# Causal masks for four pairs of heads in one GpSimd selection, and half of a zero-padded operand made by GpSimd where ScalarE made it

## The chip, the cores and the metric

The kernel runs on one core of a Trainium2 chip. The metric is the time of one execution on the device in microseconds. The engines are TensorE (PE in the profile; its weight loads are PEld), VectorE (DVE), ScalarE (ACT), GpSimd (POOL) and the DMA queues, most of which are issued by SyncE (SP).

## What is computed

Two mixers read the same `x` of 2048 rows and 512 columns, and a gate adds them row by row:

```python
g = sigmoid((x * gate_w).sum(-1, keepdims=True))
# A: Fourier mixing, real part
a = x @ dft_hid_re.T;  b = x @ dft_hid_im.T
A = dft_seq_re @ a - dft_seq_im @ b
# B: attention with 32 heads of 16 columns, each row looks at itself and the 255 rows before it
q, k, v = heads(x @ wqkv)
s = q @ k.T * 16 ** -0.5
s = where(0 <= row - col < 256, s, -1e9)
B = merge(softmax(s) @ v) @ wo
out = g * A + (1 - g) * B
```

All data are float32. Most products are made as three products of a high and a low part (`hi`, `lo`).

## The kernel before

**Two streams on one TensorE.** The attention loop in the body of the kernel runs over `n` and is the frame. The dense work (projections, Fourier products) is a Python generator, `dense()`; between two attention matmuls the loop calls `fill(n)`, which takes the next few dense matmuls from it. TensorE's order is that of the program text (`manual_schedule`); the order on the other engines is set by the scheduler, so that a change in one place can move instructions elsewhere. Each engine works its queue in order.

**The attention.** There are 4 groups of 8 heads (4 pairs `p`), and in each group 32 blocks of 64 rows: 128 blocks, numbered `n` and, 20 blocks later, `k = n - LAG`. A block is taken twice.

- *S pass*, `s_pair(n, p)`: 64 query rows of two heads against up to 320 keys, one matmul (line 325). VectorE adds the mask and takes the row minimum (line 327), ScalarE takes the exponential and sums it (line 330). Only the row maximum and the sum are kept. `ml_rows` (lines 335 to 344) writes them out, and `m_ring` puts the maxima as extra rows beneath `ring[0]`.
- *T pass*, `t_pair(k, p)`: 64 keys of two heads against up to 320 queries, one matmul (line 388), with the maxima taken off through the extra rows. ScalarE writes the exponential to `pt` (line 389), which has four buffers. After each odd pair, GpSimd sets the two triangles outside the window to zero with `affine_select`: for each half of the partitions one selection at the front of the strip (line 394) and, if the strip is 320 wide, one at its end (line 398). One selection covers 64 partitions, two pairs and 64 columns: 128 elements a partition.
- *PV*, `pv(j)`: after the third pair of every third block `k` (`k % 3 == 0`) the matmuls of the blocks `k-3`, `k-2`, `k-1` with V (line 415), which read the masked `pt`. V comes from DRAM by two DMAs for four blocks (`v_load`), and GpSimd spreads it into `vpad` (`v_spread`, line 378).

**The pads.** The two heads of a pair lie in the same partitions, 16 rows each in turn. `make_pad(i, n)` makes the weights of a block: four pairs of 64 columns for head 0 and 64 for head 1, with the other head's rows set to zero by a factor of 0 or 1 per partition (`half`). `i = 0` is for the S pass, `i = 1` for the T pass. Both halves of the S pad and the first half of the T pad are made by VectorE (line 310), the second half of the T pad by ScalarE (line 308). There are two buffers of each; the pad of block `k+1` is called for after the first pair of block `k`, and can be written when the last T matmul of block `k-1` has read its buffer.

**PSUM.** The S and T matmuls and a few others share four banks (`ps_a`); the dense products have two (`ps_d`), PV has two (`ps_o`). A matmul waits until VectorE or ScalarE has read what was in its bank.

**Dense evictions** that come up below: `split_psum` (lines 84, 86 and 88) writes a product as a high part (ScalarE) and a low part (VectorE); `split` (lines 80 and 81) does the same for weights that were loaded.

Of the kernel before, what the change touches and what calls it, by code (L numbers as in the profile page):

```python
# [9 lines left out]
AF = mybir.ActivationFunctionType  # L10
OP = mybir.AluOpType
# [7 lines left out]
NG = 4  # L19
NP = 4  # L20
BQ = 64
NB = S // BQ
# [10 lines left out]
def fnet_window_mix(ctx: ExitStack, tc: tile.TileContext, xT, x, wqk, wv, wr, wi, cr, ci, wo, gw, out):  # L33
    nc = tc.nc
# [23 lines left out]
    def f(ap):  # L58
        return ap.bitcast(F32)
# [7 lines left out]
    @contextmanager  # L67
    def behind(*engines):
        with ExitStack() as es:
            for e in engines:  # L70
                if e in last:
                    es.enter_context(tc.issue_after(last[e]))
            yield
# [51 lines left out]
    with tc.manual_schedule(engines={mybir.EngineType.Activation, mybir.EngineType.DVE, mybir.EngineType.SP}):  # L125
# [12 lines left out]
        for dk in range(DK):  # L138
            c = slice(dk * 256, dk * 256 + 256)
# [22 lines left out]
    half = const.tile([P, 2], F32, name="half")  # L162
    mrow = const.tile([P, 2], F32, name="mrow")
    for t, edges in ((half, ((0, 16, 32, 48, 64, 80), (16, 32, 48, 64, 80, 96))), (mrow, ((96, 98), (98, 100)))):
        nc.gpsimd.memset(t, 0.0)
        for h in range(2):
            for i, e in enumerate(edges[h]):
                a = t[:, h:h + 1]
# [130 lines left out]
    def make_pad(i, n):  # L299
        if not 0 <= n < NG * NB:  # L300
            return
        t = pads[i][n % NPAD]
        b = n % NB
        with behind(*(("act", "dve") if n < NPAD else ())):
            for h in range(2):
                src, dst = f(ring[i][:96, :, b * BQ:(b + 1) * BQ]), t[:96, :, 64 * h:64 * h + 64]
                if i and h:
                    nc.scalar.activation(dst, src, AF.Copy, scale=half[:96, h:h + 1])  # L308
                else:
                    nc.vector.tensor_scalar(dst, src, half[:96, h:h + 1], None, op0=OP.mult)  # L310
        PAD[i, n] = t
# [69 lines left out]
    def t_pair(n, p):  # L381
        q0 = n % NB * BQ
        w = min(WIN, S - q0)
        if p == 0:
            PT[n] = at.tile([P, NP, WIN], F32, name="pt", bufs=4)
        pt = PT[n]
        ps = ps_a.tile([P, 512], F32, name="t", tag="st")
        nc.tensor.matmul(ps[:, :w], PAD[1, n][:, p], ring[0][:, p, q0:q0 + w], start=True, stop=True)  # L388
        nc.scalar.activation(pt[:, p, :w], ps[:, :w], AF.Exp, scale=-1.0)  # L389
        if p % 2:  # L390
            ph = slice(p - 1, p + 1)
            for h in (0, 64):
                a = pt[h:h + 64, ph, 0:64]
                nc.gpsimd.affine_select(a, a, pattern=[[0, 2], [1, 64]], compare_op=OP.is_ge, fill=0.0,  # L394
                                        base=0, channel_multiplier=-1)
                if w == WIN:
                    a = pt[h:h + 64, ph, 256:320]
                    nc.gpsimd.affine_select(a, a, pattern=[[0, 2], [-1, 64]], compare_op=OP.is_gt, fill=0.0,  # L398
                                            base=0, channel_multiplier=1)

    def pv(n):
# [310 lines left out]
    for n in range(N + LAG + 2):  # L712
# [14 lines left out]
        if n == 0:  # L727
            make_pad(0, 0)
        for p in range(NP):
            if n < N:  # L730
                s_pair(n, p)
            fill(n)
            if 0 <= k < N:
                t_pair(k, p)
            if p == 0:
                make_pad(0, n + 1)
                if k >= -1:
                    make_pad(1, k + 1)
            fill(n)
            if p == 2 and sent < maxima and n >= taken[sent] + 2:  # L740
                m_ring(sent)
                sent += 1
            if p == 2 and k % 3 == 0:
                for j in range(k - 3, k):
                    if 0 <= j < N:
                        pv(j)
                if maxima < 16 and n > 8 * maxima + 8:
                    ml_rows(maxima)
                    maxima += 1
                    taken.append(n)  # L750
# [47 lines left out]
```

## Time and profile before

| | us |
|---|---|
| median of 3 runs | 871.07 |
| lowest and highest of them | 869.48, 871.13 |
| the profiled execution | 873.39 |
| its span, first to last instruction | 871.3 |

The profile is of the profiled execution, which took 873.39 us, of which 871.3 lie between the first and the last instruction. In a group's row stand the line, the engine, the operation, the tiles and shapes, the count, then the busy time and the mean duration in ns, then the idle time of the engine ahead of these instructions with what ended most of it. In a timeline's row stand the start and the duration in us, and in brackets the idle time ahead of it with what ended it. In a chain's row stand the start and the length in us of a piece of the chain that ended last. In a row of stages stand the stretch, its length, and for PE, PEld, DVE, ACT and POOL the busy time with the number of instructions, then the granted clock of TensorE, the busy share of the DMA engines and GB/s.

The T pass begins at 106.5 us and ends at 752, the S pass ends at 660; what is left is dense work and the output projection.

### The profile page before, as it was taken

The numbers are of one execution on the slowest core, as the hardware profiler recorded it, in microseconds if no ns is written. First come the engines' busy times: TensorE is split into PE (matmuls) and PEld (weight loads), VectorE is DVE, ScalarE is ACT, GpSimd is POOL, SyncE is SP. The second block draws the span as 40 slices with busy tenths as digits, with TensorE's granted clock in tenths as the row PEclk, the third lists the DMA queues.
The fourth block names the chain that finished last, engine by engine and source line by source line (L and its number), as shares of the span: only waits on it lengthen the run. The fifth ranks groups of instructions, "written<-read, shape, count | busy, mean of one in ns | idle before, by whom it ended". The sixth has DMA issues, their size and how long they took to land.

```text
span 871.3 us, 17146 instructions
## 1 busy us (share of the span) xinstructions
PE 860.5 (99%) x5160; PEld 690.3 (79%) x5160; DVE 611.3 (70%) x1974; ACT 580.9 (67%) x1793; POOL 384.6 (44%) x1067
## 2 busy tenths in 40 slices
PE   8999999999999999999999999999999999999998
PEld 6888778787877778878788887878778787788886
DVE  4588987667878987878787777788876444564431
ACT  4388799888897987878788777877776454111110
POOL 9100054545444756656456566554546665200000
PEclk9999999999999999999999999999999999999999
DMA  6875796464749436644445354599944333485541
GB/s 229 266 226 155 248 262 197 153 214 158 241 158 289 130 105 225 172 130 135 134 131 170 105 163 133 156 349 256 329 148 159 123 118 114 130 263 192 189 145 48
DMA packets 93132, 157.87 MB, mean 181 GB/s; under 512 B 27120, under 2 KB 36080, under 8 KB 93040
## 3 DMA queue, kind: packets, MB, share of 16 engines
q1 hardware_dynamic: 92288, 155.61, 56.5%
q10 hardware_dynamic: 752, 1.18, 0.4%
q8 instruction: 40, 0.66, 0.3%
q14 instruction: 52, 0.43, 0.2%
HBM read 106.69 MB, written 50.07 MB: 180 GB/s over the span
## 4 chain that ended last, share of the span: by engine, by line
PE 92%; DVE 3%; DMA 2%; ACT 1%; issue 1%; SPq 0%; DVEq 0%; ACTq 0%
PE dc L446 40%; PE dab L266 9%; PE s L325 8%; PE o L415 8%; PE dqk L244 8%; PE t L388 8%; PE t L669 5%; PE dv L266 4%; DVE sm L327 1%; PE s L232 1%; DMA raw<-x 1%; ACT sm L330 1%; DMA ring<-qk_scr 1%; PE s L337 1%; DMA pt<-xT 0%
## 5 line engine op out<-in xcount | busy, mean ns | idle before, releaser
L446 PE MATMUL dc<-big,hi 128*128 128x512 f32 x1024 | 355.4, 395 | 0.0
L394 POOL TENSOR_SCALAR_AFFINE_SELECT pt<-pt 64x128 f32<-64x128 f32 x512 | 191.9, 375 | 276.4 <-ACT pt L389 261.2
L330 ACT ACTIVATE sm<-sm,ml 128x320 f32<-128x320 f32 (+4 forms) x512 | 277.3, 543 | 49.4 <-DVE ml L327 48.0
L327 DVE CUSTOM_DVE_ANT_0 sm<-s,mask 128x320 f32<-128x320 f32 (+4 forms) x512 | 230.7, 462 | 82.7 <-PE s L325 62.5
L389 ACT ACTIVATE pt<-t 128x320 f32<-128x320 f32 (+4 forms) x512 | 208.7, 412 | 89.8 <-PE t L388 86.2
L446 PEld LDWEIGHTS dc<-big,hi 128*128 128x128 f32 x1024 | 186.3, 188 | 32.6 <-issue 2.4
L446 PE MATMUL dc<-big,lo 128*128 128x512 f32 x512 | 201.6, 394 | 0.0
L398 POOL TENSOR_SCALAR_AFFINE_SELECT pt<-pt 64x128 f32<-64x128 f32 x448 | 161.9, 361 | 0.1
L325 PE MATMUL s<-ring,pad 128*128 128x320 f32 (+4 forms) x512 | 159.0, 310 | 0.9 <-DVE ml L327 0.5
L388 PE MATMUL t<-ring,pad 128*128 128x320 f32 (+4 forms) x512 | 155.1, 303 | 1.6 <-DVE ml L327 0.9
L310 DVE TENSOR_SCALAR pad<-ring,half 96x256 fp32r<-96x256 f32 x384 | 121.6, 358 | 24.2 <-PE t L388 22.0
L325 PEld LDWEIGHTS s<-ring,pad 128*128 128x128 f32 x512 | 96.0, 188 | 36.6 <-issue 7.4
L388 PEld LDWEIGHTS t<-ring,pad 128*128 128x128 f32 x512 | 96.1, 188 | 21.6 <-DVE ml L327 2.6
L446 PEld LDWEIGHTS dc<-big,lo 128*128 128x128 f32 x512 | 96.3, 188 | 10.6
L81 DVE TENSOR_TENSOR lo<-raw,hi 128x512 fp32r<-128x512 f32 x146 | 99.6, 712 | 1.4 <-PE dc L446 1.3
L330 ACT ACTIVATION_READ_ACCUMULATOR sm<-sm,ml 128x1 f32 x512 | 98.8, 193 | 0.0
L266 PE MATMUL dab<-hi,big 128*128 128x512 f32 x256 | 90.9, 396 | 0.0
L244 PE MATMUL dqk<-big,hi 128*128 128x512 f32 x240 | 86.7, 394 | 0.6 <-DVE hl L86 0.5
L80 DVE CAST hi<-raw 128x512 fp32r<-128x512 f32 x142 | 58.6, 453 | 38.3 <-PE dc L446 37.1
L415 PE MATMUL o<-pt,vpad 128*32 128x320 f32 (+4 forms) x1408 | 73.8, 351 | 0.0
L378 POOL COPY vpad<-vr 64x256 f32<-64x256 f32 x64 | 26.0, 405 | 91.1 <-DMA vr<-v_scr 72.0
L308 ACT ACTIVATE pad<-ring,half 96x256 fp32r<-96x256 f32 x128 | 64.1, 500 | 0.0
(82 smaller groups left out, 780.3 us busy)
## 6 DMA issues: line engine op xcount, KB each, us to landing
qk_scr<-hl SPq DMA_DIRECT2D x32, 512.0 KB
ring<-qk_scr SPq DMA_DIRECT2D x32, 512.0 KB
raw<-cr SPq DMA_DIRECT2D x32, 512.0 KB
raw<-ci SPq DMA_DIRECT2D x32, 512.0 KB
ab_scr<-hl SPq DMA_DIRECT2D x20, 512.0 KB
big<-ab_scr SPq DMA_DIRECT2D x20, 512.0 KB
r_scr<-ev SPq DMA_DIRECT2D x36, 256.0 KB
ev<-r_scr SPq DMA_DIRECT2D x36, 256.0 KB
```

The costliest lines, as they stand in the source:

```text
L244: nc.tensor.matmul(ps, w[a][:, c:c + 128], XT[dk, ss][:, b], start=n == 0, stop=n == 11)
L266: nc.tensor.matmul(ps, XT[dk, ss][:, a, c * 128:(c + 1) * 128], wh[b], start=n == 0, stop=n == 11)
L310: nc.vector.tensor_scalar(dst, src, half[:96, h:h + 1], None, op0=OP.mult)
L325: nc.tensor.matmul(ps[:, :w], PAD[0, n][:, p], ring[1][:, p, k0:k0 + w], start=True, stop=True)
L327: mark("dve", nc.vector.tensor_tensor_reduce(out=sm[:, :w], in0=ps[:, :w], in1=mask[:, WIN - w:], scale=1.0, scalar=3e38, op0=OP.add, op1= ...
L330: mark("act", nc.scalar.activation(sm[:, :w], sm[:, :w], AF.Exp, bias=nm[:, c], scale=-1.0, accum_out=l[:, c]))
L388: nc.tensor.matmul(ps[:, :w], PAD[1, n][:, p], ring[0][:, p, q0:q0 + w], start=True, stop=True)
L389: nc.scalar.activation(pt[:, p, :w], ps[:, :w], AF.Exp, scale=-1.0)
L394: nc.gpsimd.affine_select(a, a, pattern=[[0, 2], [1, 64]], compare_op=OP.is_ge, fill=0.0, base=0, channel_multiplier=-1)
L398: nc.gpsimd.affine_select(a, a, pattern=[[0, 2], [-1, 64]], compare_op=OP.is_gt, fill=0.0, base=0, channel_multiplier=1)
L415: nc.tensor.matmul(OT[g, sb][32 * p:32 * p + 32, q - sb * 512:e - sb * 512], v2[:, p], pt[:, p, q - q0:e - q0], start=first, stop=kb == 8 ...
L446: nc.tensor.matmul(ps, w[a][:, i % 8 * 128:i % 8 * 128 + 128], ab[SC[i]][:, b], start=i == ends[0] and a + b == 0, stop=i == ends[1] and a ...
```

## The change

The second half of the T pad is made by GpSimd with `tensor_scalar`, as VectorE makes the first, where ScalarE made it with a scaled copy. And in two of three blocks (`n % 3 != 2`, the last block left out) the masks are set once for all four pairs, after the last pair, so that a selection covers 256 elements a partition, and there are half as many; in the other blocks, whose PV comes soonest, the masks are set after each odd pair as before.

```diff
             for h in range(2):
                 src, dst = f(ring[i][:96, :, b * BQ:(b + 1) * BQ]), t[:96, :, 64 * h:64 * h + 64]
                 if i and h:
-                    nc.scalar.activation(dst, src, AF.Copy, scale=half[:96, h:h + 1])
+                    nc.gpsimd.tensor_scalar(dst, src, half[:96, h:h + 1], None, op0=OP.mult)
                 else:
                     nc.vector.tensor_scalar(dst, src, half[:96, h:h + 1], None, op0=OP.mult)
@@
         nc.scalar.activation(pt[:, p, :w], ps[:, :w], AF.Exp, scale=-1.0)
-        if p % 2:
-            ph = slice(p - 1, p + 1)
+        joint = n % 3 != 2 and n < NG * NB - 1
+        if p == 3 or p == 1 and not joint:
+            c = 4 if joint else 2
+            ph = slice(p + 1 - c, p + 1)
             for h in (0, 64):
                 a = pt[h:h + 64, ph, 0:64]
-                nc.gpsimd.affine_select(a, a, pattern=[[0, 2], [1, 64]], compare_op=OP.is_ge, fill=0.0,
+                nc.gpsimd.affine_select(a, a, pattern=[[0, c], [1, 64]], compare_op=OP.is_ge, fill=0.0,
                                         base=0, channel_multiplier=-1)
                 if w == WIN:
                     a = pt[h:h + 64, ph, 256:320]
-                    nc.gpsimd.affine_select(a, a, pattern=[[0, 2], [-1, 64]], compare_op=OP.is_gt, fill=0.0,
+                    nc.gpsimd.affine_select(a, a, pattern=[[0, c], [-1, 64]], compare_op=OP.is_gt, fill=0.0,
                                             base=0, channel_multiplier=1)
```

In the changed program the lines behind line 389 have moved by two: the selections stand in lines 396 and 400, PV in line 417, and the output projection in line 671. TensorE, as the comparison of the two programs' orders shows, gets the same matmuls in the same order.

## The prediction

> **What bounds the kernel now.** I read the page first: busy shares, then the shares of the chain of work that ended last, then the groups of the instructions that the change touches.
>
> ```profile
> span 871.3 us, 17146 instructions
> ...
> PE 860.5 (99%) x5160; PEld 690.3 (79%) x5160; DVE 611.3 (70%) x1974; ACT 580.9 (67%) x1793; POOL 384.6 (44%) x1067
> ...
> PE 92%; DVE 3%; DMA 2%; ACT 1%; issue 1%; SPq 0%; DVEq 0%; ACTq 0%
> ...
> L394 POOL TENSOR_SCALAR_AFFINE_SELECT pt<-pt 64x128 f32<-64x128 f32 x512 | 191.9, 375 | 276.4 <-ACT pt L389 261.2
> ...
> L310 DVE TENSOR_SCALAR pad<-ring,half 96x256 fp32r<-96x256 f32 x384 | 121.6, 358 | 24.2 <-PE t L388 22.0
> ...
> L398 POOL TENSOR_SCALAR_AFFINE_SELECT pt<-pt 64x128 f32<-64x128 f32 x448 | 161.9, 361 | 0.1
> ...
> L378 POOL COPY vpad<-vr 64x256 f32<-64x256 f32 x64 | 26.0, 405 | 91.1 <-DMA vr<-v_scr 72.0
> L308 ACT ACTIVATE pad<-ring,half 96x256 fp32r<-96x256 f32 x128 | 64.1, 500 | 0.0
> ```
>
> PE carries 92% of the chain. GpSimd and ScalarE are 44% and 67% busy, so taking work from them shortens nothing by itself: only what PE loses while it waits can be won. PE's instruction order is the same in both programs (the comparison of their orders shows no moved row). So the second view is PE's busy time by stage, and the third the chain's long pure stretch, for PE's undisturbed rate.
>
> ```profile
> 105.00:128.00 23.00, 22.30 (x120) 17.02 (x121) 20.77 (x70) 21.34 (x69) 11.47 (x33) 1.00 0.93 266
> 128.00:660.00 532.00, 529.65 (x3463) 423.64 (x3462) 421.34 (x1468) 439.52 (x1408) 290.71 (x830) 1.00 0.59 183
> ```
> ```profile
> 758.84 21.12 PE dc L446 x92
> ```
>
> In the two stages with attention PE is idle for 0.70 and 2.35 us, at full clock (1.00). A matmul of 512 columns follows the last one after 21.12 / 92 = 0.23 us while its own record is 0.40 long, so a visible idle time hides 0.17 more, and the matmul behind it takes 0.41 instead of 0.31. With some eight such waits, all that could be won is about 3.05 + 8 x 0.27 = 5.2 us. The waits of the T matmuls (line 388), where the moved pad is read, and of the PV matmuls (line 415), where the masks are needed (columns: us, times):
>
> ```profile
>   DVE ml L327: 3.5, 9
>   ACT pt L389: 1.5, 4
>   ACT pad L308: 1.4, 2
> ```
> ```profile
>   POOL pt L398: 1.6, 5
> ```
>
> These are idle times of the weight load, which runs ahead of the matmuls; PE itself loses part of them. GpSimd is almost never what PE waits for, and VectorE, which the change leaves its work, is waited for most.
>
> **The change part by part.** *ScalarE* loses 128 pads of 0.50 us: 64.1 us, from 580.9 to 517. That counts only where a pad stands in front of something PE waits for. I found four places.
>
> (a) The first T matmul, at 106.5:
>
> ```profile
> 106.06 0.41 ACT pad L308
> ```
> ```profile
> 106.52 0.41 PE L388 MATMUL t<-ring,pad 128*128 128x320 f32 x1 [0.52 <-ACT pad L308]
> ```
> ```profile
> 109.66 1.45 DVE L81 TENSOR_TENSOR lo<-raw,hi 128x512 fp32r<-128x512 f32 x2
> 111.67 0.39 PE L388 MATMUL t<-ring,pad 128*128 128x320 f32 x1 [0.18 <-DVE ml L327]
> ```
>
> The loss is 0.52 + 0.17 + 0.10 = 0.8 us. On GpSimd the first two pads wait only for loads and are ready early, so it goes. But what is late next is VectorE, which has a backlog here (20.77 of 23 us busy) and holds PE at 111.67 whether PE comes early or not. I count the 0.8 as given back there: 0.
>
> (b) At 213 PE waits for line 86, which stands behind line 81 on VectorE:
>
> ```profile
> 212.50 0.68 DVE L81 TENSOR_TENSOR lo<-raw,hi 128x512 fp32r<-128x512 f32 x1
> 213.10 0.68 DVE L86 TENSOR_TENSOR hl<-dqk,hl 128x512 fp32r<-128x512 f32 x1
> ```
> ```profile
> 213.84 0.73 PE L244 MATMUL dqk<-big,hi 128*128 128x512 f32 x2 [0.53 <-DVE hl L86]
> ```
>
> In the changed program's order line 86 stands ahead of line 81 and of one pad at this place, so it comes at least 0.6 us sooner: the 0.53 + 0.16 + 0.10 = 0.8 us go.
>
> (c) At 302 and (d) at 576 a pad stands in the row of ScalarE's instructions that ends in PE's wait:
>
> ```profile
> 300.91 0.50 ACT L308 ACTIVATE pad<-ring,half 96x256 fp32r<-96x256 f32 x1
> ```
> ```profile
> 302.33 0.41 PE L325 MATMUL s<-ring,pad 128*128 128x320 f32 x1 [0.31 <-ACT pt L389]
> ```
> ```profile
> 576.05 0.40 ACT pad L308
> ...
> 579.25 0.41 PE s L325
> ```
> ```profile
> 578.80 0.40 PE L446 MATMUL dc<-big,lo 128*128 128x512 f32 x1
> ```
>
> (c) loses 0.31 + 0.17 + 0.10 = 0.58; the pad holds the chain for 0.40, so 0.5 go with the restart. (d) loses 579.25 - 578.80 - 0.23 = 0.22 and 0.10; 0.3 go. For waits too small to show on PE (4 times 1.5 us of the weight load on line 389) I take another 0.3, between 0 and 0.8. ScalarE's part: -0.8 - 0.5 - 0.3 - 0.3 = -1.9 us.
>
> *The masks.* Of 128 blocks 85 become joint: 75 with four selections and 10, at the ends of the groups, with two, 320 of 256 elements; the other 43 keep 37 x 8 + 6 x 4 = 320 of 128. Before there were 960. A selection's price by size:
>
> ```profile
> L153 POOL TENSOR_SCALAR_AFFINE_SELECT mask<-mask 64x320 f32<-64x320 f32 x2 | 0.9, 450 | 0.1
> ```
> ```profile
> 119.69 0.39 POOL L378 COPY vpad<-vr 64x256 f32<-64x256 f32 x1 [4.30 <-DMA vr<-v_scr]
> 120.39 0.45 POOL L378 COPY vpad<-vr 64x256 f32<-64x256 f32 x1 [0.31 <-DMA vr<-v_scr]
> 120.91 0.29 POOL L394 TENSOR_SCALAR_AFFINE_SELECT pt<-pt 64x128 f32<-64x128 f32 x1
> ...
> 124.13 0.30 POOL L398 TENSOR_SCALAR_AFFINE_SELECT pt<-pt 64x128 f32<-64x128 f32 x1
> ```
> ```profile
> 120.53 0.31 PE L388 MATMUL t<-ring,pad 128*128 128x320 f32 x1
> 123.58 1.82 PE L415 MATMUL o<-pt,vpad 128*32 128x320 f32 x24
> ```
>
> 0.29 at 128 and 0.45 at 320 elements give 0.40 at 256. With the means' stretch of 375 / 290 = 1.29 all masks come to 320 x 0.40 x 1.29 + 320 x 0.37 = 283 us, 71 below the 354 of lines 394 and 398.
>
> *The pad on GpSimd* has no row. Nearest is the copy of 256 elements, 0.40 alone (405 mean); upper end 1.3, a short mask's time beside a busy VectorE; lower end 0.3, the same mask alone:
>
> ```profile
> 610.45 1.30 POOL L394 TENSOR_SCALAR_AFFINE_SELECT pt<-pt 64x128 f32<-64x128 f32 x1
> ```
>
> I take 0.42: 54 us, GpSimd 385 - 71 + 54 = 368. The Trainium skill ("GPSIMD Engine Reference", section "Engine selection") advises against elementwise work there: about half VectorE's speed with two inputs, roughly line rate with one. By its worse figure the pad would take 2 x 0.358 = 0.72 (an estimate), and the sum would be 0.6 worse; no run here shows it yet.
>
> What hides it in the steady stage: a pad may start when the T matmuls two blocks back are done, and GpSimd then idles for the exponentials (261 us in all). Around the PV group at 246:
>
> ```profile
> 244.01 0.29 POOL L394 TENSOR_SCALAR_AFFINE_SELECT pt<-pt 64x128 f32<-64x128 f32 x1 [1.57 <-ACT pt L389]
> ...
> 244.84 0.30 POOL L398 TENSOR_SCALAR_AFFINE_SELECT pt<-pt 64x128 f32<-64x128 f32 x1
> 246.31 1.23 PEld L415 LDWEIGHTS o<-pt,vpad 128*32 128x32 f32 x24 [0.36 <-issue]
> ```
>
> The pad falls into the 1.57 us. Behind it in GpSimd's queue stand the masks of the block whose last T matmul it waits for, and these wait for that matmul's exponential, which comes later still. The masks end at 245.14, 1.2 us ahead of the group and 2.3 ahead of its third block, the only one that reads them. The third block of each group keeps its masks in two parts, and the joint ones are read a block later. Cost: 0. The wait for GpSimd that T matmuls now carry is a wait for something long done; 0.
>
> At the start it isn't hidden. GpSimd's queue stands until the V loads land (119.69, 120.39). Before, half of block 1's masks were done ahead of that; in the changed order all of block 1's stand behind both copies and one pad, and a second pad stands ahead of block 2's last masks. From 120.39: pads and copies to 120.95, four joint masks 1.6, four short 1.2, a pad 0.4, four short 1.2: 125.4, to 125.9 with VectorE's stretch, instead of 124.43. The third PV block starts at 123.58 + 1.82 x 2/3, less the tail of the last record, about 124.7. PE is held by 0.7 to 1.2: +0.9. The pad between the two copies ends at 120.5, just when PE wants it at 120.53: inside that sum.
>
> **Sum:** -1.9 + 0.9 = -1.0. The profiled execution took 873.39 us for its span of 871.3; it would take 872.4. The median of the unprofiled runs is 871.07, 2.3 below; there I forecast **870.1**, with a range of its own from 868.9 to 871.3 (the start between +0.5 and +1.5, ScalarE's part between -2.7 and -1.2).
>
> **The rivals.**
>
> *1. The relief is larger.* (a) is kept because VectorE also runs ahead, the V loads land sooner as PE does, and a part of the DVE waits (3.5 us) goes since ScalarE frees buffers sooner. For it: 64 us off an engine that is 440 of 532 us busy. Against: VectorE's own load stays. Price: -0.8 for (a), no start cost, -1.9, -0.9 of the DVE waits: -3.6, **867.5**.
>
> *2. GpSimd becomes late: slower.* Its pads stand in order ahead of masks. If one takes 1.3 us, two more at the start cost 1.8; and the five PV groups that already wait for a mask are held about 0.3 longer each, 1.5 together. +0.9 + 1.8 + 1.5 - 1.9 = +2.3, **873.4**. It decides from about 1.1 us a pad. For it: masks average 375 against 290 alone. Against: the copy, as large, averages 405. The skill's same page (section "Specifications") says GpSimd shares its SBUF interface with VectorE, with contention when VectorE runs a 2-port mode or two SBUF inputs; the stretched masks agree with it.
>
> *3. It does not do what it says.* PE's order is unchanged, and each freed wait turns into one for VectorE within a block, as at (a), while the start's loss and the gain at (b) cancel: **871.1**.
>
> **How the numbers follow.** A difference under 0.2% (1.7 us) is about what a measurement of this kernel cannot tell from none. Forecast 0.53, of which 0.11 lies below 869.3; rival 1 0.24; rival 2 0.13; rival 3 0.10. Faster 0.11 + 0.24 = 0.35; same 0.42 + 0.10 = 0.52; slower 0.13. The range 867.4 to 872.9 leaves out half of rival 1 and most of rival 2, some 0.2.
>
> **What would show it.** After the change: no ACT row of line 308, 128 GpSimd rows of it with a mean near 0.42; GpSimd's masks near 283 us; the PE waits at 106, 213 and 302 gone; a new wait of line 417's matmuls for GpSimd near 125 of about 0.9; PE still waiting near 111 for VectorE. The forecast is wrong if the pad's mean is above 1 us, if T matmuls wait for GpSimd in the steady stage, or if the PE waits of VectorE shrink as well.

## The result, and the profile after

The changed kernel is slower: 876.01 us (median of 6 runs, 874.0 to 876.69) against 870.11 us (868.44 to 871.13) for the kernel before on the same chip, a ratio of 1.0065 with a 95% interval of 1.0049 to 1.0081. The forecast was 870.1. The profiled execution of the changed kernel took 876.69 us for a span of 875.0.

The page of the changed kernel, the lines that answer to those of before:

```profile
span 875.0 us, 16814 instructions
...
PE 863.1 (99%) x5160; PEld 689.3 (79%) x5160; DVE 631.0 (72%) x1974; ACT 541.0 (62%) x1665; POOL 451.5 (52%) x875
...
PE 91%; DVE 3%; DMA 2%; issue 2%; POOL 1%; ACT 0%; SPq 0%; DVEq 0%; POOLq 0%
...
L308 POOL TENSOR_SCALAR pad<-ring,half 96x256 fp32r<-96x256 f32 x128 | 142.0, 1109 | 151.2 <-PE t L388 136.6
...
L396 POOL TENSOR_SCALAR_AFFINE_SELECT pt<-pt 64x256 f32<-64x256 f32 (+1 forms) x342 | 145.6, 426 | 34.7 <-ACT pt L389 22.6
...
L310 DVE TENSOR_SCALAR pad<-ring,half 96x256 fp32r<-96x256 f32 x384 | 143.6, 414 | 22.1 <-PE t L388 20.7
...
L400 POOL TENSOR_SCALAR_AFFINE_SELECT pt<-pt 64x256 f32<-64x256 f32 (+1 forms) x298 | 131.0, 439 | 0.0
```

Read the mean of line 308 first: a pad on GpSimd takes 1.109 us, not 0.42. GpSimd's work has grown from 384.6 to 451.5 us where the forecast had it fall to 368. The masks came out as forecast: 145.6 + 131.0 = 276.6 us (283 foreseen). And VectorE's own pads, which nobody touched, went from 358 to 414 ns, 384 times: 22.0 us more on the engine that PE waits for most.

Where did PE lose the time? The stages of the two kernels, before and then after (stretch, length, busy time of PE, PEld, DVE, ACT and POOL with counts, granted clock, DMA share, GB/s):

```profile
0.00:15.00 15.00, 11.27 (x32) 8.26 (x33) 9.00 (x14) 7.00 (x13) 13.88 (x23) 0.89 0.61 199
102.00:128.00 26.00, 25.25 (x134) 19.22 (x133) 23.77 (x79) 23.27 (x76) 11.47 (x33) 1.00 0.90 264
...
268.00:660.00 392.00, 390.18 (x2537) 311.58 (x2536) 317.96 (x1102) 318.26 (x1018) 225.12 (x608) 1.00 0.59 180
```
```profile
0.00:15.00 15.00, 13.03 (x47) 9.63 (x48) 8.65 (x16) 8.07 (x15) 13.75 (x25) 1.00 0.66 222
102.00:128.00 26.00, 23.51 (x116) 16.97 (x116) 19.93 (x68) 18.90 (x60) 11.09 (x22) 0.93 0.84 248
...
268.00:660.00 392.00, 388.66 (x2521) 308.33 (x2520) 330.10 (x1091) 291.45 (x932) 263.89 (x489) 1.00 0.59 178
```

The first row is a trap. In before's profiled execution the clock was at 0.89 in the first 15 us and PE did 32 matmuls there, not 47; that execution is some 3.3 us late ahead of anything that the change touches. So positions are compared from the first T matmul on. It stands at 106.52 less its wait of 0.52 in before, so at 106.00, and at 102.63 after. What counts then is the second row, the start of the T pass: 116 matmuls in 26 us, not 134. It shows the place and not the size, since the T pass begins 3.4 us later in before's window; the size is counted from the first T matmul on.

GpSimd's timeline of the changed kernel there (start, duration, what ended the idle time ahead of it), and then PE's:

```profile
117.50 0.48 POOL L378 COPY vpad<-vr 64x256 f32<-64x256 f32 x1 [7.51 <-DMA vr<-v_scr]
117.97 0.91 POOL L308 TENSOR_SCALAR pad<-ring,half 96x256 fp32r<-96x256 f32 x1
118.94 0.40 POOL L378 COPY vpad<-vr 64x256 f32<-64x256 f32 x1
119.41 0.41 POOL L396 TENSOR_SCALAR_AFFINE_SELECT pt<-pt 64x256 f32<-64x256 f32 x1
...
122.31 0.92 POOL L308 TENSOR_SCALAR pad<-ring,half 96x256 fp32r<-96x256 f32 x1
123.19 0.46 POOL L396 TENSOR_SCALAR_AFFINE_SELECT pt<-pt 64x128 f32<-64x128 f32 x1
...
124.73 0.74 POOL L400 TENSOR_SCALAR_AFFINE_SELECT pt<-pt 64x128 f32<-64x128 f32 x1
```
```profile
102.63 0.39 PE L388 MATMUL t<-ring,pad 128*128 128x320 f32 x1
...
118.94 0.42 PE L388 MATMUL t<-ring,pad 128*128 128x320 f32 x1 [1.78 <-POOL pad L308]
...
123.16 2.14 PE L417 MATMUL o<-pt,vpad 128*32 128x320 f32 x20
125.53 0.73 PE L417 MATMUL o<-pt,vpad 128*32 128x320 f32 x4 [0.23 <-POOL pt L400]
126.91 0.31 PE L388 MATMUL t<-ring,pad 128*128 128x320 f32 x1
```

GpSimd stands idle for 7.51 us with a V copy at the head of its queue, until the load lands at 117.50. Behind that copy stands the pad of block 3 (0.91), for which PE waits 1.78 us. Then come the second copy, the masks of block 1, half those of block 2, the pad of block 4 (0.92), and the last masks of block 2, which end at 125.47. The third PV block needs these. PE comes to the T matmul behind that PV group at 126.91 - 102.63 = 24.28 us after the first T matmul. In before it came there at 126.05 - 106.00 = 20.05:

```profile
126.05 0.31 PE L388 MATMUL t<-ring,pad 128*128 128x320 f32 x1
```

The start has lost 4.2 us, where the medians of all runs differ by 5.9. From here to the last T matmul, which begins at 751.95 in before and at 755.65 after, the profiled execution loses 2.8 us more (628.74 for 625.90).

### The profile page after: what moved, and what is told of

Read it like the earlier page. It is cut to its first block, busy times and chain, and to the rows that moved or that the text cites. A ratio compares the mean times of both kernels' runs of the same rounds, so it can differ in the third digit from the quotient of the medians.

```text
span 875.0 us, 16814 instructions
## 1 busy us (share of the span) xinstructions
PE 863.1 (99%) x5160; PEld 689.3 (79%) x5160; DVE 631.0 (72%) x1974; ACT 541.0 (62%) x1665; POOL 451.5 (52%) x875
## 4 chain that ended last, share of the span: by engine, by line
PE 91%; DVE 3%; DMA 2%; issue 2%; POOL 1%; ACT 0%; SPq 0%; DVEq 0%; POOLq 0%
PE dc L448 39%; PE dqk L244 9%; PE dab L266 9%; PE s L325 9%; PE o L417 8%; PE t L388 8%; PE dv L266 5%; PE t L671 5%; DVE sm L327 1%; DVE pad L310 1%; DMA big<-ab_scr 1%; PE s L337 1%; DMA ab_scr<-hl 1%; DVE lo L81 1%; PE s L232 0%
## 5 line engine op out<-in xcount | busy, mean ns | idle before, releaser
L308 POOL TENSOR_SCALAR pad<-ring,half 96x256 fp32r<-96x256 f32 x128 | 142.0, 1109 | 151.2 <-PE t L388 136.6
L396 POOL TENSOR_SCALAR_AFFINE_SELECT pt<-pt 64x256 f32<-64x256 f32 (+1 forms) x342 | 145.6, 426 | 34.7 <-ACT pt L389 22.6
L310 DVE TENSOR_SCALAR pad<-ring,half 96x256 fp32r<-96x256 f32 x384 | 143.6, 414 | 22.1 <-PE t L388 20.7
L400 POOL TENSOR_SCALAR_AFFINE_SELECT pt<-pt 64x256 f32<-64x256 f32 (+1 forms) x298 | 131.0, 439 | 0.0
```

Of the source, the lines that this page charges most:

```text
L308: nc.gpsimd.tensor_scalar(dst, src, half[:96, h:h + 1], None, op0=OP.mult)
L396: nc.gpsimd.affine_select(a, a, pattern=[[0, c], [1, 64]], compare_op=OP.is_ge, fill=0.0, base=0, channel_multiplier=-1)
```

## The experiments

My theory after the result: GpSimd's pad is dear, and it costs time at this one place, where two pads stand in GpSimd's queue among masks and behind a load. Rivals: the joint masks come too late for PV; the price is paid all along, through VectorE's stretched pads. Ratios are to the kernel before in runs on the same chip, with 95% intervals; in brackets the medians.

**1. The pads alone on GpSimd, the masks as before.** Only the first hunk of the diff.

> Only the pad moves to GpSimd; the masks stay in selections of two pairs. Theory A (the pad is what costs: 1.0 us each on GpSimd, one of them behind the V loads at the start, and VectorE's own pads stretched): +4 to +7 us against the kernel before, line 308 near 1.1 us, line 310 near 0.41 us, a T matmul waiting for line 308 near 117 us. Theory B (the joint masks come too late): within 1 us of before. Theory C (only the start costs): +3 to +4 us.

Measured: 1.0043, 1.0027 to 1.0059 (874.29 us). PE's waits for GpSimd (total, times, longest):

```profile
PE o L415 <- POOL pt L398: 1.4, 1, 1.4
...
PE t L388 <- POOL pad L308: 0.9, 1, 0.9
```

Two waits, both at the start, where the clock was full (1.00):

```profile
102.00:128.00 26.00, 23.11 (x120) 16.95 (x120) 20.99 (x72) 19.90 (x62) 14.73 (x35) 1.00 0.89 256
```

PE comes to the T matmul behind the PV group 126.28 - 103.18 = 23.10 us after the first one, against 20.05 in before: 3.05 of the 4.2 us. The pads alone do most of the harm. By time, 0.43% or 3.7 us, the run lies in theory C's range and just under theory A's.

**2. The joint masks alone, the pads on ScalarE.** Only the second hunk.

> Only the joint masks; ScalarE keeps the pad. Theory A: within 1 us of before, GpSimd near 320 us busy, PE held at the start by at most 0.5 us. Theory B: +4 to +7 us, with PV matmuls waiting for line 400. Theory C: within 1 us.

Measured: 1.0012, 1.0000 to 1.0024 (872.25 us), with no wait of PE for GpSimd. That the joint masks come too late for PV isn't what costs 5.9 us: they cost 1.0 us (0 to 2.1).

**3. The first five T pads on ScalarE again.**

```diff
-                if i and h:
+                if i and h and n < 5:
+                    nc.scalar.activation(dst, src, AF.Copy, scale=half[:96, h:h + 1])
+                elif i and h:
                     nc.gpsimd.tensor_scalar(dst, src, half[:96, h:h + 1], None, op0=OP.mult)
```

> The changed kernel, but ScalarE makes the T pads of blocks 0 to 4, so that no pad stands in GpSimd's queue around the V loads at the start. Theory A: the wait of 1.8 us near 117 goes and 3 to 4 us come back; +2 to +3 us against before stay, as VectorE's pads stay stretched (line 310 near 0.41 us) and PE waits for VectorE at 458, 536, 577, 614 and 642 us stay. Theory C: all of it comes back, -1 to +0.5 us against before. Theory B: +5 us stay.

Measured: 1.0014, 1.0004 to 1.0023 (872.13 us). Five of 128 pads carry 1.0065 - 1.0014 = 0.51%, 4.4 us. The other 123 take as long as ever (1109 ns in the mean). What stays against before, 1.2 us (0.3 to 2.0), is less than theory A's 2 to 3 and more than theory C's 0.5.

**4. GpSimd copies its pad half instead of multiplying** (this leaves out the zeroing of the other head's rows).

```diff
-                    nc.gpsimd.tensor_scalar(dst, src, half[:96, h:h + 1], None, op0=OP.mult)
+                    nc.gpsimd.tensor_copy(dst, src)
```

> The changed kernel, but GpSimd copies the second half of the T pad and does not multiply it by the factor of 0 or 1, so that the other head's rows are left in. It measures what the multiplication costs on GpSimd. Theory A: line 308 falls from 1.1 us to 0.42 us, line 310 goes back to near 0.36 us; the wait at the start shrinks by 0.6 us and the later waits for VectorE mostly go: +1 to +3 us against before. If the size and not the operation sets the price, line 308 stays at 1 us and the time at +6 us.

Measured: 1.0009, 0.9996 to 1.0021 (871.12 us). The groups of the pad and of VectorE's pads:

```profile
L310 DVE TENSOR_SCALAR pad<-ring,half 96x256 fp32r<-96x256 f32 x384 | 134.4, 390 | 22.9 <-PE t L388 21.2 <-DMA ring<-qk_scr 1.2
L308 POOL CAST pad<-ring 96x256 fp32r<-96x256 f32 x128 | 64.9, 507 | 170.6 <-PE t L388 159.1 <-DMA ring<-qk_scr 7.2 <-issue 1.6
```

At half the price and in the same place, most of the loss is gone. The two pads that count at the start take 0.39 and 0.65 us, near the 0.42 that I had put into the sum, and even so the run is 0.8 us slower than before (-0.3 to +1.8) where the sum had -1.0, and a little under theory A's 1 to 3. VectorE's pads go back only half the way (390 ns, 358 before). In its profiled execution (872.55 us) PE still waits for GpSimd at the start, 0.37 us for a pad and 1.38 for the masks, and the T matmul behind the PV group comes 125.50 - 103.05 = 22.45 us after the first one: 2.4 us lost there, where the sum had 0.9.

**5. GpSimd multiplies by the constant 1.0** instead of by the column of factors (leaves out the same zeroing).

```diff
-                    nc.gpsimd.tensor_scalar(dst, src, half[:96, h:h + 1], None, op0=OP.mult)
+                    nc.gpsimd.tensor_scalar(dst, src, 1.0, None, op0=OP.mult)
```

> The changed kernel, but GpSimd multiplies its half of the T pads by the constant 1.0 instead of by the factors of the rows, read from a column of memory (it leaves out the zeroing of the other head's rows). If it is the read column that makes the pad 0.91 us where a copy of the same tile takes 0.51 us in the run with copies: the pad falls to about 0.5 us and the time to 871 to 872 us. If it is the multiplication itself: the pad stays near 1.1 us in the mean and the time at 875 to 877 us.

Measured: 1.0042, 1.0027 to 1.0058 (874.22 us).

```profile
L308 POOL TENSOR_SCALAR pad<-ring 96x256 fp32r<-96x256 f32 x128 | 121.2, 947 | 156.9 <-PE t L388 144.6 <-DMA ring<-qk_scr 7.0 <-issue 1.6
```

947 ns, against 1109 with the column and 507 for the copy: most of the price is the multiplication itself on this engine, the read column is the smaller part. The mean lies between the two that were expected, and the time just under the 875 to 877 us of the second.

**6. Only the two pads on ScalarE that stand in the way**, those of blocks 3 and 4 (`if i and h and n in (3, 4):` in the diff of experiment 3).

> The changed kernel, but ScalarE makes its half of two T pads again, those of blocks 3 and 4; GpSimd keeps the other 126. My theory (two pads at the start cost nearly all: the one behind the V copies, for which the T matmul of block 3 waits 1.8 us, and the next one, which stands ahead of the masks of block 2): 871.7 to 872.8 us, as with the first five pads on ScalarE, and no wait of a T matmul for GpSimd over 0.2 us. Rival (the price is paid all along, a little in every block): 875 to 876.5 us.

Measured: 1.0019, 1.0010 to 1.0029 (871.91 us), and PE waits for GpSimd nowhere. Two pads of 128 account for 0.46%, 4.0 us.

**7. All pads on GpSimd, but nothing queued behind the load.** The copies of the second V load are put behind the first pads and masks (`mark` notes an instruction, `behind` makes the next ones follow it).

```diff
-                    nc.gpsimd.tensor_scalar(dst, src, half[:96, h:h + 1], None, op0=OP.mult)
+                    mark("pool", nc.gpsimd.tensor_scalar(dst, src, half[:96, h:h + 1], None, op0=OP.mult))
...
-            nc.gpsimd.tensor_copy(v2[r, :, :, 16 * h:16 * h + 16], raw[r].rearrange("r j (p d) -> r j p d", d=16))
+            with behind(*(("pool",) if n == 4 else ())):
+                nc.gpsimd.tensor_copy(v2[r, :, :, 16 * h:16 * h + 16], raw[r].rearrange("r j (p d) -> r j p d", d=16))
```

The two selections are marked in the same way.

> The changed kernel with all pads on GpSimd, but the copies of the second V load are put behind the pads and masks of the first blocks in GpSimd's order, so that nothing of these waits for the load. If the start's loss comes from the order (a pad and the masks queued behind a load that lands at 117.5): no T matmul waits for GpSimd, the masks of block 2 end some 3 us earlier, and the time is 871.5 to 872.8 us. If it comes from the sum of GpSimd's work at the start, whatever its order: 874 to 876 us.

Measured: 1.0012, 1.0001 to 1.0024 (871.58 us). GpSimd's timeline, and then the T matmuls around the PV group:

```profile
112.00 0.92 POOL L308 TENSOR_SCALAR pad<-ring,half 96x256 fp32r<-96x256 f32 x1 [1.97 <-PE t L389]
...
116.94 0.92 POOL L308 TENSOR_SCALAR pad<-ring,half 96x256 fp32r<-96x256 f32 x1 [0.54 <-PE t L389]
...
118.86 0.29 POOL L401 TENSOR_SCALAR_AFFINE_SELECT pt<-pt 64x128 f32<-64x128 f32 x1
119.22 0.85 POOL L379 COPY vpad<-vr 64x256 f32<-64x256 f32 x2
```
```profile
102.67 0.39 PE L389 MATMUL t<-ring,pad 128*128 128x320 f32 x1
...
120.34 1.82 PE L418 MATMUL o<-pt,vpad 128*32 128x320 f32 x24
122.81 0.31 PE L389 MATMUL t<-ring,pad 128*128 128x320 f32 x1
```

The same two pads at the same 0.92 us are now made 6.0 and 5.4 us earlier, in time that GpSimd had spent standing behind a V copy whose load had not landed; block 2's masks end at 119.15 and not at 125.47. PE comes to the T matmul behind the PV group 122.81 - 102.67 = 20.14 us after the first one, against 20.05 in before. So the start's loss goes with the order alone, as it goes in experiment 6 with the two pads alone: it takes both, the pad's price and its place behind the load.

**8. The pads again apart from VectorE's**, to see whether the stretch of VectorE's pads is the rest of the loss. On the basis of experiment 3, GpSimd's half is called for two pairs of heads later from block 5 on.

```diff
-                    make_pad(1, k + 1)
+                    make_pad(1, k + 1, (0, 1) if k < 4 else (0,))
+            if p == 2 and k >= 4:
+                make_pad(1, k + 1, (1,))
```

> The changed kernel with the first five T pads on ScalarE (872.13 us), and from block 5 on GpSimd's half is issued two pairs of heads later than VectorE's half, so that they no longer run side by side. Theory of the shared memory path (VectorE's pads are stretched from 0.36 to 0.41 us by GpSimd's, and that is the rest of the loss, about 1.2 us): VectorE's pads fall to 0.36 to 0.38 us in the mean and the time to 870.7 to 871.5 us. Rival (the rest of the loss has another cause, or the stretch only passes to VectorE's other work): 871.8 to 873 us, with the pads shorter all the same.

Measured: 1.0021, 1.0010 to 1.0032 (872.27 us), VectorE's pads 414 ns. It tells nothing of the question: the scheduler places the pad by when its buffer is free, and the order on every engine is that of experiment 3. As a repeat of that kernel it gives 1.0021 for 1.0014, which shows how far the steady part can be read. One thing differs: PE waits 0.79 us for a mask in its first PV group, with no pad of GpSimd ahead of it, and in experiment 3's profile it does not. There the V copies began 13.18 us after the first T matmul, here 13.76.

**9 to 11. What is left, taken apart.** The order edit of experiment 7 on the pads alone, on the masks alone, and on the kernel before.

> The pads alone on GpSimd, masks as before, with the copies of the second V load put behind the pads and masks of the first blocks. With the copies in their old place the pads alone cost 0.43%. If the order at the start is what makes the pads dear: a ratio of 0.9990 to 1.0020 (869.1 to 871.8 us). If the eight short masks of block 2, 2.4 us instead of the joint ones' 1.7 us in each block, hold the start as well: 1.003 or more. The rest of the loss of the repaired kernel (0.12%) belongs to the pads if this run shows about 1.0010 and the masks alone show 1.0000.

> The joint masks alone, ScalarE's pads as before, with the copies of the second V load behind the masks of the first blocks. If the joint masks cost nothing but their place at the start: 0.9990 to 1.0006. If the rest of the repaired kernel's loss (0.12%) is the masks': about 1.0012.

> The kernel before, with the copies of the second V load behind the masks of the first blocks and nothing else. Nothing waits for GpSimd at the start of the kernel before, so the order alone should be worth nothing: 0.9992 to 1.0008. If the order itself gains or costs time, this run shows how much of the repaired kernels' times is the order's.

Measured: the pads alone 1.0003, 0.9994 to 1.0012 (870.23 us); the masks alone 1.0006, 0.9998 to 1.0015 (870.14 us); the kernel before 1.0000, 0.9991 to 1.0008 (869.79 us). The order by itself is worth nothing, and with it each edit costs nothing that can be told from zero. With their old order the pads alone had cost 0.43%.

**12. Each GpSimd pad from block 5 on written twice**, on the basis of experiment 7 (`for _ in range(2 if n >= 5 else 1):` ahead of the marked pad).

> The repaired kernel (all pads on GpSimd, second V copies behind the first masks; ratio 1.0012), with each of GpSimd's pads from block 5 on written twice. If GpSimd's pads cost time in the steady part through VectorE, whose own pads run beside them: VectorE's pads go above 0.43 us in the mean and the time to 873 us or more (1.003). If the steady part has room for 1.1 us more a block on GpSimd and the loss lies elsewhere: 871 to 872 us (1.001 to 1.002).

Measured: 1.0150, 1.0136 to 1.0163 (882.8 us); by the ratios 1.38%, some 12 us, more than experiment 7.

```profile
PE t L390 <- POOL pad L309: 3.8, 10, 0.6
PE t L390 <- DVE ml L328: 2.6, 6, 1.5
```
```profile
L311 DVE TENSOR_SCALAR pad<-ring,half 96x256 fp32r<-96x256 f32 x384 | 143.8, 415 | 22.2 <-PE t L390 20.8 <-DMA ring<-qk_scr 0.8
```

VectorE's pads do not stretch further, but now T matmuls wait for the pad in the steady part, ten times. So there is room there for one pad of 1.1 us a block, or nearly, and not for two. The second half of the expectation, that the loss lies elsewhere and a second pad is free, is refuted. Of the first half the time came true and the longer pads of VectorE did not. VectorE's `ml` is late too: PE's waits for it at this line were 0.6 us, 2 times, in experiment 7. The waits shown are about half of the 12 us, and the rest was not traced.

## Why the prediction was wrong, step by step

- **"I take 0.42" for the pad on GpSimd: the step that failed.** A pad alone takes 0.91 to 0.92 us and 1.109 in the mean. I took the row of a copy of the same size; experiment 4 shows that a copy costs about that (0.39 us alone, 507 ns in the mean), and experiment 5 that the multiplication doesn't. My upper bound of 1.3 held it, and a mean above 1 us was one of my own signs of being wrong. The Trainium skill ("GPSIMD Engine Reference", section "Engine selection") puts one-input work there at roughly line rate: measured, this one-input multiplication takes 0.92 us alone where VectorE's takes 0.36 in the mean of before, and the measurement decides. Its figure of twice VectorE's time, for two inputs, was the better guess.
- **"The pad between the two copies ends at 120.5, just when PE wants it: inside that sum", and T matmul waits of 0.** Measured: 1.78 us in the changed kernel, 0.9 and 1.2 in experiments 1 and 5. Half a microsecond of it is the pad's price; in the profile of the changed kernel the load also landed later, 117.50 - 102.63 = 14.87 us after the first T matmul against 119.69 - 106.00 = 13.69 in before. In the other profiles with the copies in their old place it lies, counted without the first T matmul's own wait, between 13.6 (experiment 6) and 14.4 (experiment 5), so the late landing may be the chance of this execution.
- **The start, "+0.9".** Measured 4.2 in the profile. From the first copy to block 2's last mask I had 125.9 - 119.69 = 6.2 us; it took 125.47 - 117.50 = 8.0. Of the 1.8 more, two pads at 0.91 and 0.92 for 0.42 are 1.0, and the last four masks, 2.28 us where I had 1.2 and 0.5 of stretch, 0.6. The later load adds 1.2. With my own gross 125.9 - 124.7 = 1.2 these are 4.2. The place, the queue and the instruction that PE waits for at 125 were right; the size was not. And the pad's price is not all of it: with the copy of experiment 4 the start still loses 2.4 us. My sum left next to nothing between the load's landing and PE's need.
- **VectorE, "which the change leaves its work".** Its instructions stayed, their durations didn't: 358 to 414 ns for the pads.
- **ScalarE's part, -1.9: (b) is there, the rest is not, and the pads cost time in the steady part that I had put at 0.** The waits named did go: no T matmul waits for a pad of ScalarE, and the stages of the repaired kernel (experiment 7) show (b):

```profile
128.00:268.00 140.00, 139.96 (x931) 112.46 (x930) 108.63 (x367) 113.96 (x364) 82.11 (x181) 1.00 0.59 192
268.00:660.00 392.00, 390.06 (x2531) 310.49 (x2532) 331.31 (x1097) 293.76 (x940) 268.14 (x497) 1.00 0.57 178
```

  Up to 268 PE is idle for 0.04 us, where this row of before has 0.53:

```profile
128.00:268.00 140.00, 139.47 (x929) 112.06 (x927) 103.38 (x367) 121.27 (x391) 65.59 (x222) 1.00 0.59 191
```

  After 268 nothing is won (1.94 idle, 1.82 before). Much of the freed time turned into ScalarE waiting for VectorE. The exponentials of the S pass, before and after:

```profile
L330 ACT ACTIVATE sm<-sm,ml 128x320 f32<-128x320 f32 (+4 forms) x512 | 277.3, 543 | 49.4 <-DVE ml L327 48.0
```
```profile
L330 ACT ACTIVATE sm<-sm,ml 128x320 f32<-128x320 f32 (+4 forms) x512 | 277.0, 542 | 76.9 <-DVE ml L327 73.7
```

  ScalarE's busy time fell by 39.9 us (580.9 to 541.0, and not to 517: the records of its instructions overlap, so 128 x 0.50 is more than the pads had taken), and its waits for `ml` grew by 26. That is rival 3's mechanism, a freed wait that becomes a wait for VectorE; the pads with the order repaired (experiment 9) are at +0.3 us, -0.5 to +1.0, and not at -1.9.
- **The masks** were right: 0.41 us for a joint one alone (0.40 foreseen), and their cover in the steady part holds. PE waited for a mask once, at 125.
- **Rival 2** had the right engine, with 873.4 for 876.0. Its threshold ("from about 1.1 us a pad") was too high: experiment 5's pads take 947 ns in the mean, and that kernel is 0.42% slower; and the two that count in the changed kernel took 0.91 and 0.92. Two of its terms were off: the two pads at the start cost about 4 and not 1.8 + 0.9, and no PV group behind the first waited for a mask. I gave it 0.13 because I priced the pad by the copy.

**What stays open.** The four runs in which the start is repaired and both edits are in (experiments 3, 6, 7 and 8) give 1.0012 to 1.0021, so 1.0 to 1.8 us are still lost. Each edit alone, repaired, shows 1.0003 and 1.0006 with intervals that hold zero, and these two add up to 0.09%, less than 0.8 us. Part of the loss can be placed, since PE does the same matmuls in the same order everywhere. The first rows of two PV groups of before, and of the same two in experiment 7:

```profile
447.30 1.13 PE L415 MATMUL o<-pt,vpad 128*32 128x64 f32 x20
555.16 1.84 PE L415 MATMUL o<-pt,vpad 128*32 128x256 f32 x48
```
```profile
443.19 1.40 PE L418 MATMUL o<-pt,vpad 128*32 128x64 f32 x24
551.76 1.84 PE L418 MATMUL o<-pt,vpad 128*32 128x256 f32 x48
```

Before takes 107.86 us from one to the other, experiment 7 takes 108.57. The profiled executions with GpSimd multiplying its pads once take 108.42 to 108.67 (the changed kernel, experiments 1, 3 and 5 to 9), those with copies or with the pads on ScalarE 107.82 to 107.94 (experiments 2, 4, 10 and 11). So the multiplying pads cost 0.6 to 0.8 us here, where I had put the steady part at 0; in experiment 9 the gains, that at (b) among them, hide it. How they cost it isn't shown. VectorE's own pads are longer in all of these (407 to 419 ns), and in experiment 4, which loses nothing here, they take 390; that this is the cause was only argued. The rest of the loss isn't placed: the profiled execution of experiment 7 was the fastest of its 12 (870.07 us), and that of experiment 8 lost part at the start. PE's idle time between 268 and 660 can't decide it: it is 1.82 us in before's profile and 392.00 - 388.96 = 3.04 in experiment 11, which is the same work at the same time.

```profile
268.00:660.00 392.00, 388.96 (x2533) 311.23 (x2532) 316.78 (x1099) 317.71 (x1017) 225.66 (x612) 1.00 0.58 178
```

No version that was run beats the kernel before.

## What to carry to other kernels

When an operation moves to another engine, price it by a row of that operation on that engine; a copy of the same size was half its price, and if no such row exists, the decision belongs at the upper bound. Then look for the places where that engine's queue stands still behind a load: what is queued there waits for the load as well and can cost more than its own time (here two pads of 0.92 us cost about 4), and putting the load's consumer behind the urgent work takes that cost away (here 4.6 of 5.7 us, by the ratios). An engine that has idle time on average and is off the critical path can still set the end at the one place where its queue starts late.

## What the runs showed of the hardware

- **VectorE and GpSimd stretch each other.** Sorted by what GpSimd does meanwhile, VectorE's 384 pads of the changed kernel take 345 ns with GpSimd idle (62 of them) and 452 ns with more than half of their time beside a pad of GpSimd (195). It goes the other way too: GpSimd's pads take 0.95 us in the mean beside VectorE's pads alone (33 of them), and 1.55 where line 81 runs meanwhile (24). Two rows of VectorE and one of GpSimd in the changed kernel:

```profile
405.67 0.61 DVE L310 TENSOR_SCALAR pad<-ring,half 96x256 fp32r<-96x256 f32 x2
406.19 1.28 DVE L81 TENSOR_TENSOR lo<-raw,hi 128x512 fp32r<-128x512 f32 x2
```
```profile
405.90 2.55 POOL L308 TENSOR_SCALAR pad<-ring,half 96x256 fp32r<-96x256 f32 x1 [0.73 <-PE t L388]
```

  This pad takes 2.55 us where one takes 0.92 alone. The Trainium skill ("GPSIMD Engine Reference", section "Specifications") says that the two share their SBUF interfaces and contend when VectorE has two SBUF inputs, as line 81 has; these rows agree.
- **Behind a short stall of PE the half clock was granted once.** Behind PE's wait of 1.78 us at 117, the granted clock of the changed kernel's profiled execution was 0.50 (the figure behind POOL's count) for some 3.4 us:

```profile
120.50:123.80 3.30, 3.30 (x16) 2.03 (x18) 2.09 (x7) 2.41 (x7) 3.09 (x9) 0.50 0.58 204
```

  The Trainium skill ("TensorE: Matmul & The Clock Gate", part 1) names an idle window of about 3.4 us for that; here PE was never idle that long. A stall of this length doesn't always do it: experiment 11 has a longer one, and its clock stayed at 1.00, so what brought the half clock isn't shown.

```profile
277.98 0.41 PE L389 MATMUL t<-ring,pad 128*128 128x320 f32 x1 [1.83 <-DVE ml L327]
```

  It isn't what makes the kernel slow: the PV group waited for its masks to 125.47 anyway, experiment 1 has its two waits at a clock of 1.00, and another execution of the changed kernel took 876.66 us at a mean clock of 1.00.
